# Row sum by an accumulating addition, squares on ScalarE, more transposes by DMA, the last tile in two halves, and a new order

## The chip, the cores and the metric

The kernel runs on one core of a Trainium2 chip. Its time is the device time in microseconds (us). The four compute engines are TensorE (PE in the profile, with its weight loads as PEld), VectorE (DVE), ScalarE (ACT) and GpSimd (POOL); SyncE (SP) issues most of the DMAs.

## What is computed

Inputs are r, k and v of shape (4 batches, 8 heads, 768 steps, 48), decays w and bonuses u per head and channel, and the weights of a two-layer network. The first part is a linear attention with a decaying state, the second a normalised network with a residual:

```python
for t in range(S):
    cur = np.einsum('bhd,bhe->bhde', u[None] * kt, vt)
    y[:, :, t] = np.einsum('bhd,bhde->bhe', rt, state + cur)
    state = w[None, :, :, None] * state + np.einsum('bhd,bhe->bhde', kt, vt)
# x: y as (B, S, H * D) = (4, 768, 384)
mu = np.mean(x, axis=-1, keepdims=True)
var = np.mean((x - mu) ** 2, axis=-1, keepdims=True)
xn = (x - mu) / np.sqrt(var + 1e-06) * g_ln
ch = np.maximum(xn @ w_ch1, 0.0) @ w_ch2        # 384 -> 1536 -> 384
return (x + ch).astype(np.float32)
```

## The kernel before

The 3072 rows (4 x 768) are cut into 24 tiles of 128 rows, six to a batch. A tile i passes through these steps, each a small function of the program whose name stands in the plan:

- `LK`, `LR`, `LV` (L315 to L322) load the tile's k, r and v, each 192 KB in runs of 192 bytes, through SP's queue into rings of ten buffers.
- `SK`, `SR` (through `times`, L203) scale k and r by powers of the decay into bf16 (`sck`, `scr`); `CV` casts v into `vv`.
- `TR` (L338) transposes `scr` and `sck` on TensorE, four 128x128 blocks each, into a PSUM tile `tr`; `TC`, or `TCr` and `TCk` apart, copies it to `trs` (r in half 0, k in half 1). For tiles in `K_BY_DMA` (18 to 23) only r is transposed so, and `TKD` (L477) brings k with a DMA transpose from `sck` to `trs`, issued on SP's queue.
- `Q` multiplies the two halves of `trs`; `AT` (L357) makes the 128x128 products of k and r per head; `AM` masks them into `A`; `S` (L388 to L401) makes the bonus terms and the state's increment; `CC`, `ZU`, `ZD` update the state `Z`; `VB` (L420) multiplies v by the bonus terms; `Y` (L430, L438) is the attention's output in PSUM. For tiles in `ZPE` (1 to 3) the old state is added in `S` by one matmul with the identity (L395), and then `ZU` alone makes the new state; otherwise `ZU` adds on VectorE and `ZD` multiplies on GpSimd.
- `X` (L445) adds `Y` and `Vb` to `x`. `ST` (L448) and `AG` (L452) take mean and variance of its rows; `XN` (L458, L460) writes mean minus x as bf16 into `xn`; `RS` (L466, L469) makes the inverse standard deviation on GpSimd.
- `LT` (L482) transposes `xn` on TensorE in three blocks and `XT` copies the result to `xT`.
- `UP` (L497) multiplies by the first weights, `RL` (L513, L515) applies the relu into `hT`, `DN` (L525) multiplies by the second weights, four matmuls of 384 columns to a step and three steps to a tile; `OT` (L535) scales and adds x, and `STO` (L542) stores 192 KB.

`GROUPS` says how many tiles share one pass of `UP`: one for tiles 0 to 7 and 20 to 23, two for 8 to 19. A step `UP,i` or `RL,i` belongs to group i // 16 and block i % 16; a step `DN,i` to tile i // 4.

At the start `LN`, `WBM`, `FK`, `FR` make the powers of the decay (`Fk`, `Fr`), `LG` loads the gain vector and `UGC` negates it, `LW1` and `IW2` load the two weight matrices in three parts each, and `SW` casts parts of the first to bf16 with the gain in them. `WU` and `DU` are matmuls of zeros that do no work of the reference.

The order of everything is one list, `PLAN`. It is walked from left to right; each entry is a step, its number and an engine letter (v VectorE, s ScalarE, g GpSimd, - where the step has only one). An engine runs its own instructions in this order, and waits on semaphores where a step needs another engine's result. SP's queue is one such order as well: loads, DMA transposes and stores stand in it one behind the other. In the listing of the program a DMA on it also waits for the landing of an earlier one, since eight semaphores are used in turn for DMAs issued by SP and ScalarE.

```python
for step in PLAN.split():
    name, i, e = step.split(",")
    steps[name](int(i), e)
```

Of the kernel before, what the change touches and what calls it, by code (L numbers as in the profile page):

```python
# [7 lines left out]
FP32 = mybir.dt.float32  # L8
# [87 lines left out]
def kernel(  # L96
# [347 lines left out]
    def X(i, e):  # L444
        nc.vector.tensor_tensor(out=xx(i)[:], in0=psum["y", i][:, :C], in1=Vb(i)[:], op=ALU.add)  # L445

    def ST(i, e):
        nc.vector.bn_stats(out=stats[i % 4][:], in_=xx(i)[:])  # L448

    def AG(i, e):  # L450
        g, j, _ = group_of[i]
        nc.vector.bn_aggr(out=mv[g][:, j, :], in_=stats[i % 4][:])  # L452
# [130 lines left out]
```

## Time and profile before

Three runs took 156.22, 157.09 and 157.25 us; the median is 157.09 us. The profile is of another execution of the same program:

| | |
|---|---|
| the profiled execution's own time | 156.55 us |
| its span, from the first instruction to the last | 154.4 us |
| outside the span | 2.15 us |
| PE, DVE, ACT, POOL busy | 146.4, 119.4, 76.2, 95.7 us |
| mean granted TensorE clock | 0.996 |
| matmuls | 1926, of them 105 of zeros |

"Busy" is the time in which at least one instruction of the engine was running. Matmuls overlap each other, so their own durations (219 ns for one of 128 columns) are longer than the distance at which they follow each other; that distance is read from the chain of waits or from the timeline, where eight transposes take 0.45 us. Lines of a helper (L198, L200, L203) stand for several steps, which the tile names tell apart.

### The profile page before, as it was taken

What the parts mean: (1) busy time and instruction counts of PE and PEld (TensorE: products, weight loads), DVE (VectorE), ACT (ScalarE), POOL (GpSimd) and SP (SyncE); (2) the same over time, 40 slices, a digit from 0 to 9 for tenths busy, and PEclk for the clock granted to TensorE, in tenths of its full rate; (3) what the DMA queues carried; (4) which work ended last, traced back from release to release, by engine and by line L of the source; (5) the groups of instructions that cost most, each with busy time, mean ns of one, the idle gap of its engine ahead of it and who ended that gap; (6) DMA issues with size and microseconds to landing.
All of it is one profiled execution on the core that took longest, in us unless ns stands there. A gap on an engine that the chain in (4) does not pass through costs nothing.

```text
span 154.4 us, 4697 instructions
## 1 busy us (share of the span) xinstructions
PE 146.4 (95%) x1926; PEld 118.6 (77%) x1926; DVE 119.4 (77%) x242; ACT 76.2 (49%) x149; POOL 95.7 (62%) x135
## 2 busy tenths in 40 slices
PE   7689999999899999999999999999999999999990
PEld 4488788868677887979688878877778778878770
DVE  2256989789998999999999999797797769734211
ACT  4526884434155747657535746356455244143330
POOL 3182665356749499995693698798766968333200
PEclk9999999999999999999999999999999999999998
DMA  4999999999999999989899897132153051102111
GB/s 82 192 182 354 349 200 206 210 177 212 226 200 188 199 255 179 257 170 232 170 243 208 176 261 107 51 89 34 51 87 87 0 89 51 51 20 82 56 56 51
DMA packets 84487, 23.51 MB, mean 152 GB/s; under 512 B 79857, under 2 KB 82930, under 8 KB 84466
## 3 DMA queue, kind: packets, MB, share of 16 engines
q1 hardware_dynamic: 83202, 22.03, 64.5%
q0 software_dynamic: 432, 1.18, 4.2%
q8 instruction: 15, 0.25, 0.7%
q10 hardware_dynamic: 832, 0.00, 0.3%
q14 instruction: 6, 0.05, 0.1%
HBM read 18.88 MB, written 4.72 MB: 153 GB/s over the span
## 4 chain that ended last, share of the span: by engine, by line
PE 73%; DVE 16%; DMA 3%; ACT 2%; issue 2%; SPq 1%; POOL 1%; POOLq 0%; DVEq 0%; ACTq 0%
PE o L525 27%; PE hp L497 26%; PE tr L338 5%; PE at L357 4%; DVE A L367 4%; DMA rf<-in_r_dram 3%; PE tr L482 3%; DVE scr L203 2%; PE y L438 2%; PE s L401 2%; PE y L430 2%; PE o L261 2%; DVE x L445 2%; PE s L388 1%; DVE stats L448 1%
## 5 line engine op out<-in xcount | busy, mean ns | idle before, releaser
L513 ACT ACTIVATE hT<-hp 128x512 bf16<-128x512 f32 x68 | 40.0, 597 | 49.5 <-PE hp L497 48.9
L497 PE MATMUL hp<-xT,w_sb 128*128 128x128 bf16 (+1 forms) x648 | 57.2, 237 | 0.3 <-ACT w_sb L306 0.2
L525 PE MATMUL o<-w_sb,hT 128*128 128x384 bf16 x288 | 57.1, 326 | 0.2 <-DVE hT L515 0.2
L497 PEld LDWEIGHTS <-w_sb 128*128 128x128 bf16 x648 | 49.4, 113 | 4.4 <-ACT w_sb L306 0.4
L525 PEld LDWEIGHTS <-hT 128*128 128x128 bf16 x288 | 25.3, 98 | 11.6 <-DVE hT L515 0.4
L367 DVE TENSOR_TENSOR A<-at,mask 128x1024 bf16<-128x1024 f32 (+1 forms) x26 | 29.1, 1127 | 3.3 <-PE at L357 3.3
L420 POOL TENSOR_TENSOR Vb<-vf,cc 128x384 f32<-128x384 f32 x24 | 21.6, 898 | 12.6 <-ACT cc L198 6.7
L203 POOL TENSOR_TENSOR scr<-rf,Fr 128x384 bf16<-128x384 f32 x16 | 16.2, 1019 | 11.7 <-DMA rf<-in_r_dram 8.2
L535 DVE SCALAR_TENSOR_TENSOR ot<-o,rs,x 128x384 f32<-128x384 f32 x24 | 14.7, 611 | 10.3 <-PE o L525 10.2
L445 DVE TENSOR_TENSOR x<-y,Vb 128x384 f32<-128x384 f32 x24 | 13.1, 547 | 4.2 <-POOL Vb L420 3.1
L203 POOL TENSOR_TENSOR Z<-ZS,WLZ 128x384 bf16<-128x384 f32 x13 | 13.6, 1048 | 2.5 <-DVE ZS L414 2.3
L198 ACT COPY trs<-tr 128x512 bf16<-128x512 bf16 (+1 forms) x13 | 10.0, 782 | 10.5 <-PE tr L338 10.5
L448 DVE BATCH_NORM_STATS2 stats<-x 128x6 f32<-128x384 f32 x24 | 13.3, 554 | 0.4
L203 POOL TENSOR_TENSOR sck<-kf,Fk 128x384 bf16<-128x384 f32 x12 | 12.6, 1046 | 0.3 <-PE s L401 0.3
L469 POOL TENSOR_TENSOR rs<-rs,expo 128x1 f32<-128x1 f32 (+1 forms) x18 | 10.9, 603 | 1.5
L338 PE MATMUL tr<-ident,scr 128*128 128x128 bf16 x96 | 9.7, 227 | 1.9 <-POOL scr L203 1.9
L261 PE MATMUL o<-warm 128*128 128x128 bf16 x105 | 10.3, 269 | 1.0 <-DVE warm L226 1.0
L203 DVE TENSOR_TENSOR sck<-kf,Fk 128x384 bf16<-128x384 f32 x12 | 9.6, 799 | 1.4 <-DMA kf<-in_k_dram 1.4
L203 DVE TENSOR_TENSOR q<-trs 128x512 bf16<-128x512 bf16 x18 | 8.8, 489 | 2.4 <-ACT trs L198 2.4
L261 PEld LDWEIGHTS <-warm 128*128 128x128 bf16 x105 | 8.7, 124 | 2.4 <-issue 1.3
L458 ACT ACTIVATE xn<-x,mv 128x384 bf16<-128x384 f32 x15 | 9.2, 613 | 2.5 <-DVE mv L452 2.5
L357 PE MATMUL at<-trs 48*128 48x128 bf16 x192 | 9.8, 222 | 0.4 <-DVE trs L200 0.3
(66 smaller groups left out, 180.2 us busy)
## 6 DMA issues: line engine op xcount, KB each, us to landing
kf<-in_k_dram SPq DMA_DIRECT2D x24, 192.0 KB, 3.9
vf<-in_v_dram SPq DMA_DIRECT2D x24, 192.0 KB, 4.1
rf<-in_r_dram SPq DMA_DIRECT2D x24, 192.0 KB, 3.9
out_dram<-ot SPq DMA_DIRECT2D x24, 192.0 KB, 2.5
w_f<-in_moe_w_ch_dram SPq DMA_DIRECT2D x3, 768.0 KB, 7.3
w_sb<-in_moe_w_ch_dram POOLq DMA_DIRECT2D x3, 384.0 KB, 6.5
trs<-sck SPq DMA_TRANSPOSE x6, 3.6
u_p<-in_u_dram ACTq DMA_DIRECT2D x2, 0.8 KB, 3.1
```

Of the source, the lines that this page charges most:

```text
L203: engines[e].tensor_tensor(out=out, in0=in0, in1=in1, op=ALU.mult)
L261: nc.tensor.matmul(out=warm_ps[0][:, :P], lhsT=warm[:], rhs=warm[:], start=True, stop=True)
L338: nc.tensor.transpose(out=t[:, a * HP + q, :], in_=flat[:, q, :], identity=ident[:])
L357: nc.tensor.matmul(out=t[:, par, q, :], lhsT=trs(i)[p0 : p0 + D, 1, q, :], rhs=trs(i)[p0 : p0 + D, 0, q, :], start=True, stop=True,)
L367: nc.vector.tensor_tensor(out=AA(i)[:, a:b].rearrange("p e q t -> p (e q) t"), in0=psum["at", i][:, a:b].rearrange("p e q t -> p (e q) t") ...
L420: nc.gpsimd.tensor_tensor(out=Vb(i)[:].rearrange("p (h d) -> p h d", h=H), in0=vf(i)[:], in1=cc(i)[:].unsqueeze(2).to_broadcast([P, H, D]) ...
L445: nc.vector.tensor_tensor(out=xx(i)[:], in0=psum["y", i][:, :C], in1=Vb(i)[:], op=ALU.add)
L448: nc.vector.bn_stats(out=stats[i % 4][:], in_=xx(i)[:])
L497: nc.tensor.matmul(out=t[:, a * gw : (a + 1) * gw], lhsT=w1_sb[n][kc][:, fb::FB], rhs=xT(g)[:, kc, :gw], start=(kc == 0), stop=(kc == CK - 1),
L513: nc.scalar.activation(out=o, in_=s, func=ACT.Relu)
L525: nc.tensor.matmul(out=psum["o", i][:, :C], lhsT=hT(g)[:, fk, j * P : (j + 1) * P], rhs=w2_sb[d][:, a, :], start=(fk == 0), stop=(fk == FK ...
L535: nc.vector.scalar_tensor_tensor(out=ot(i)[:], in0=psum["o", i][:, :C], scalar=rs[g][:, j : j + 1], in1=xx(i)[:], op0=ALU.mult, op1=ALU.add,)
```

## The change

Five things change, and with them the order of nearly every step.

1. `X` becomes one instruction that adds and also sums its rows into `sm`; `ST` and `AG` are gone. `XN` works with the row sum, so it writes C times what it wrote (C = 384), and the new step `SQ` on ScalarE squares that and sums it into `sq`; `RS` is made from `sq`, with the same factor C in it.
2. `K_BY_DMA` begins at 14 and not at 18; a new step `TRD` brings r by DMA for tiles 20 to 23 too, and their `TR` is gone from the plan; rows 14 to 23 of `xn` are brought to `xT` by DMA (`LTD`), and their `LT` and `XT` are gone.
3. `ZPE` takes in tile 4.
4. The last tile's `DN`, `OT` and `STO` are each cut into two halves of 192 columns: `DA`, `DB`, `OA`, `OB`, `SA`, `SB`. `DB` writes a PSUM tile of the ring of `UP`.
5. The plan is another list: steps stand elsewhere, and many have another engine. By count: `SR` has 9 on GpSimd and 15 on VectorE (16 and 8 before), `SK` 10 and 14 (12 and 12), `TC` 8 on ScalarE and 4 on VectorE (6 and 10, of 16), `Q` 9 on GpSimd (6), `XN` 8 on VectorE, 12 on ScalarE, 4 on GpSimd (3, 15, 6), `CV` 16 on ScalarE (13). The zero matmuls are 94 (105). `LG` and `UGC` stand near the front.

```diff
-ZPE = [1, 2, 3]
-K_BY_DMA = [18, 19, 20, 21, 22, 23]
+ZPE = [1, 2, 3, 4]
+K_BY_DMA = [14, 15, 16, 17, 18, 19, 20, 21, 22, 23]
...
     def X(i, e):
-        nc.vector.tensor_tensor(out=xx(i)[:], in0=psum["y", i][:, :C], in1=Vb(i)[:], op=ALU.add)
-
-    def ST(i, e):
-        nc.vector.bn_stats(out=stats[i % 4][:], in_=xx(i)[:])
-
-    def AG(i, e):
+        nc.vector.scalar_tensor_tensor(
+            out=xx(i)[:], in0=psum["y", i][:, :C], scalar=1.0, in1=Vb(i)[:], op0=ALU.mult, op1=ALU.add,
+            accum_out=sm[i][:],
+        )
+
+    def SQ(i, e):
         g, j, _ = group_of[i]
-        nc.vector.bn_aggr(out=mv[g][:, j, :], in_=stats[i % 4][:])
+        nc.scalar.activation(
+            out=sqj[:], in_=xx(i)[:], func=ACT.Square, bias=sm[i][:], scale=-float(C), accum_out=sq[g][:, j : j + 1]
+        )
...
         if e == "s":
-            nc.scalar.activation(out=xn(i)[:], in_=xx(i)[:], func=ACT.Identity, bias=mean, scale=-1.0)
+            nc.scalar.activation(out=xn(i)[:], in_=xx(i)[:], func=ACT.Identity, bias=sm[i][:], scale=-float(C))
...
         nc.gpsimd.tensor_scalar(
-            out=rs[g][:], in0=mv[g][:, :, 1], scalar1=1e-6, scalar2=1.0, op0=ALU.add, op1=ALU.mult
+            out=rs[g][:], in0=sq[g][:], scalar1=1.0 / C, scalar2=1e-6 * C * C, op0=ALU.mult, op1=ALU.add
         )
...
+    def TRD(i, e):
+        flat = scr(i)[:].rearrange("p h d -> p (h d)")
+        nc.sync.dma_start_transpose(out=trs(i)[:, 0], in_=flat)
...
+    def half(i, name, pool, c0):
+        g, j, _ = group_of[NT - 1]
+        n = FK // NW
+        if i == 0:
+            psum[name] = pool.tile([P, 512], FP32, name="o" if name == "oA" else "hp")
+        for a in range(n):
+            fk = i * n + a
+            nc.tensor.matmul(
+                out=psum[name][:, : C // 2],
+                lhsT=hT(g)[:, fk, j * P : (j + 1) * P],
+                rhs=w2_sb[i][:, a, c0 : c0 + C // 2],
+                start=(fk == 0),
+                stop=(fk == FK - 1),
+            )
...
+    def half_out(i, name, c0):
+        g, j, _ = group_of[i]
+        nc.vector.scalar_tensor_tensor(
+            out=ot(i)[:, c0 : c0 + C // 2], in0=psum[name][:, : C // 2], scalar=rs[g][:, j : j + 1],
+            in1=xx(i)[:, c0 : c0 + C // 2], op0=ALU.mult, op1=ALU.add,
+        )
...
+    def half_store(i, c0):
+        b, c = divmod(i, NCH)
+        nc.sync.dma_start(
+            out=out[b, c * L : (c + 1) * L, c0 : c0 + C // 2], in_=ot(i)[:, c0 : c0 + C // 2]
+        )
```

`LTD` was in the program before, but no plan entry used it:

```python
def LTD(i, e):
    g, j, _ = group_of[i]
    nc.sync.dma_start_transpose(out=xT(g)[:, :, j * P : (j + 1) * P], in_=xn(i)[:])
```

The beginning of the new plan, up to the first `UP`, and its end:

```
MW,0,v WF,0,- TL,0,s MI,0,g WU,13,- MM,0,g MP,0,v LN,0,s LG,0,- ROWSI,0,s WBM,0,- LR,0,-
UGC,0,s FK,0,s LK,0,- FR,0,s LR,1,- SR,0,g WL,0,s SK,0,v LK,1,- UW,0,g DU,24,- TR,0,-
SR,1,v LK,2,- TCk,0,v SK,1,v LV,0,- TCr,0,v SK,2,v DU,12,- AT,0,- LR,2,- TR,1,- CV,0,s
AMa,0,v LV,1,- Q,0,g AMb,0,v SR,2,v LW1,0,- DU,7,- Y,0,- S,0,- TCk,1,v CC,0,s TCr,1,v
CV,1,s ZU,0,v Q,1,g DU,10,- TR,2,- LV,2,- TC,2,v DU,4,- AT,1,- VB,0,g S,1,- SW,2,s
AMa,1,v LW1,1,- SW,1,g SW,0,s X,0,v Q,2,v CV,2,g XN,0,s AMb,1,v DU,20,- LT,0,- CC,1,v
SQ,0,s Y,1,- ZU,1,v LK,3,- VB,1,g AT,2,- XT,0,v SW,5,s SW,4,v RS,0,g UP,0,- LR,3,-
...
STO,17,- DN,74,- SQ,21,s Q,23,g AT,22,- LTD,21,- OT,18,v RL,226,s UP,224,- RS,15,g AM,22,v DN,76,-
RL,224,s UP,240,- ZU,22,v STO,18,- DN,77,- ZD,22,g DN,78,- S,23,- UP,225,- OT,19,v Y,22,- CC,23,v
RL,225,s VB,23,g DN,80,- X,22,v RL,240,s DN,81,- STO,19,- AT,23,- DN,82,- XN,22,v SQ,22,s AM,23,v
UP,241,- RS,16,g UP,242,- OT,20,v LTD,22,- RL,241,s Y,23,- DN,84,- X,23,v RL,242,s DN,85,- XN,23,v
STO,20,- UP,256,- DN,86,- SQ,23,s LTD,23,- UP,257,- RL,256,s RS,17,g OT,21,v UP,258,- RL,257,s DN,88,-
RL,258,s DN,89,- STO,21,- UP,272,- DN,90,- RL,272,s UP,273,- UP,274,- OT,22,v RL,273,s DA,0,- RL,274,s
DA,1,- DA,2,- DB,0,- STO,22,- DB,1,- OA,23,v DB,2,- OB,23,v SA,23,- SB,23,-
```

## The prediction

> **What bounds the kernel now.** I read the page's busy times first, then the engines by stage, then what TensorE waits for, and last the two ends of the timeline.
>
> ```profile
> PE 146.4 (95%) x1926; PEld 118.6 (77%) x1926; DVE 119.4 (77%) x242; ACT 76.2 (49%) x149; POOL 95.7 (62%) x135
> ```
>
> The table by stage (stretch, then busy us and instructions of PE, PEld, DVE, ACT, POOL, clock, DMA share, GB/s):
>
> ```profile
> 31.00:60.00 29.00, 28.44 (x434) 22.64 (x433) 27.14 (x51) 14.63 (x31) 20.52 (x26) 1.00 0.98 206
> 60.00:78.00 18.00, 17.78 (x251) 14.40 (x250) 17.62 (x35) 10.73 (x22) 14.72 (x19) 1.00 0.97 205
> 78.00:96.00 18.00, 18.00 (x229) 15.15 (x226) 17.81 (x35) 10.53 (x18) 13.24 (x17) 1.00 1.00 204
> 96.00:120.00 24.00, 24.00 (x289) 19.42 (x287) 19.07 (x39) 12.90 (x27) 18.21 (x25) 1.00 0.27 64
> 120.00:151.00 31.00, 30.88 (x368) 24.08 (x365) 16.68 (x33) 10.41 (x21) 13.87 (x20) 1.00 0.18 50
> ```
>
> From 31 us on PE is full. DVE is nearly as full until 96 us, ScalarE is half idle, and the DMA engines fall from full to a quarter once the loads are done. Who released PE after 31 us (total, times, longest):
>
> ```profile
> PE at L357 <- DVE trs L200: 0.3, 1, 0.3
> PE y L438 <- DVE A L367: 0.2, 1, 0.2
> PE o L525 <- DVE hT L515: 0.2, 1, 0.2
> ```
>
> So 0.7 us of named waits in 120: there a TensorE instruction taken away is time gained, and one that has to wait is time lost. A busy PE can hide small gaps, since matmuls overlap: by starts in the timeline I find about 1.1 us more between 39.7 and 42.8, where the chain of waits runs through DVE. Before 31 us it is different (start, duration, engine, instruction, count, idle before it):
>
> ```profile
> 4.35 0.58 ACT L275 ACTIVATE Fk<-y,pow_i 128x384 f32<-128x384 f32 x1 [1.80 <-PE y L271]
> ...
> 7.09 0.99 POOL L203 TENSOR_TENSOR scr<-rf,Fr 128x384 bf16<-128x384 f32 x1 [5.01 <-DMA rf<-in_r_dram]
> ...
> 8.13 0.61 PE L338 MATMUL tr<-ident,scr 128*128 128x128 bf16 x4 [1.85 <-POOL scr L203]
> ...
> 17.97 0.62 ACT L458 ACTIVATE xn<-x,mv 128x384 bf16<-128x384 f32 x1 [0.71 <-DVE mv L452]
> ...
> 19.43 0.83 PE L497 MATMUL hp<-xT,w_sb 128*128 128x128 bf16 x12
> ```
>
> The first transpose waits for r of tile 0, the first `UP` for tile 0's whole attention. At the other end the last `DN` ends at 150.9, and `OT` (0.62) and a store follow. DMA transposes, from the view of `trs` on SP:
>
> ```profile
> L477 SPq DMA_TRANSPOSE trs<-sck x6: 1190/1212/1947, 92.3 to 123.8; - x6
> ...
> DMA to landing us min/median/max: 2.4/3.6/4.3
> ```
>
> SP is held for 1.2 us by each; it lands 2.4 us after its issue starts if the queue is quiet, 3.6 beside a store, 4.3 beside the loads (the first, at 92.3).
>
> **The change part by part, against the profiled execution (156.55 us).**
>
> TensorE work. Gone are k's transposes of tiles 14 to 17 (16), r's of 20 to 23 (16) and ten tiles of three in `LT` (30): 62. Eight take 0.45 us in the chain, so 56 ns each: 62 x 0.056 = -3.5. Tile 4 in `ZPE` adds one matmul of 384 columns, 0.16 (four of them take 0.65): net **-3.3**. 24 half matmuls of `DA`, `DB` replace 12 whole ones at the same number of columns: 0. The zero matmuls all stand before the PE-bound stage; their removal is in the start's sum.
>
> DVE. Gone: 24 `ST` at 554 ns and 24 `AG` at 173, 17.4 us. `X` turns from 547 ns to the form of `OT`, 611: +1.5. Seven more `SR` at 766: +5.4, two `SK` at 799: +1.6, five `XN` at 597: +3.0; six fewer `TC` at 678 and six fewer `XT` at 356: -6.2; three fewer `Q` at 489: -1.5. The row sum's read-out is not in the trace. The Trainium skill ("VectorE: DVE Perf Modes", section "Two Vector instructions with no wait between them") says that an operation which also writes out its accumulator is two instructions. Nearest rows of one column: 60 ns (a memset) and 173 (`AG`); I take 100, so +2.4; without the rule it would be 0, both hidden. Sum about -11 of 119: DVE no longer runs level with PE. Cover: PE is the later of the two from 31 us, so this is worth only the gaps around 40 us. I take **-0.5** (0 to -1.1).
>
> ScalarE. 24 `SQ` at the price of `XN` (613 ns), plus a read-out between 0 and 204 ns (the small `g_neg` row of that engine): 15 to 20 us. The moves of other steps about cancel, so 76 becomes 91 to 96 of 150: its cover is the half that is idle, 48.9 us of it spent by `RL` waiting for `UP`. An `SQ` in front of an `RL` can hold it for 0.7 us, and `UP` two blocks later needs that buffer; there is mostly a `DN` (0.65) between. Taken as 0 (-0 to +1.5). GpSimd loses some 8 us net; it had 38% idle: 0.
>
> The start. `LG` is now second on SP's queue and `UGC` stands before `FK` on ScalarE. The gain vector's DMA lands after 3.2 us by its row: issued near 1.1, landed 4.3, so `FK` starts at 4.5 instead of 4.35, a loss of 0.15; `FR` and `SR` of tile 0 are behind it. r of tile 0 is now the first big load, not the third: issued near 1.6, with the median of 3.9 landed at 5.5. `SR,0` then starts at 5.6 instead of 7.09. 24 zero matmuls from 4.2 at 0.11 each end at 6.8, so the first `TR` is at 6.8 instead of 8.13. `X` to `XN` loses `ST` and `AG`, 0.7 us on the path. But ahead of `XN,0` ScalarE now does two casts of weights that arrive behind eight loads, as before: not before about 14.7, plus 1.3. So `XN,0` is near 16.3 and the first `UP` near 17.8 instead of 19.43. Then something else is late: `IW2,0` stands on POOL's queue behind `SK,3`, which waits for k of tile 3. It is issued near 20 instead of 15.65; at 5.1 to 6.5 us to landing that is 25 to 26.5, while the first `DN`, with 2.3 us more PE work in front of it, would be ready at 24.2. That gives back some of it: **-1.3** (+0.5 to -2.5).
>
> The rows by DMA. `LT` and `XT` became `LTD`: 1.2 us of SP and 2.4 to 4.3 to landing. The first `UP` of the group waits for it, in order, with all of PE behind it. The PE work in the plan between `XN` and that `UP`: tile 15 three `DN`, `TR` of r, `AT`, `Y`, `S` = 1.95 + 0.22 + 0.33 + 0.37 + 0.27 = 3.1; likewise 17: 3.4, 19: 3.2, 20: 4.2, 21: 3.0, 22: 3.0, 23: 4.0. In the trace of before the real distance is 0.3 to 0.8 longer than counted so (tile 23: 1.47 counted, 142.36 to 144.13 in the timeline); with 0.5 the margins are 3.6, 3.9, 3.7, 4.7, 3.5, 3.5, 4.5. Needed: `XN` 0.6, a semaphore, and the landing: 3.05 quiet, 4.25 beside a store, 4.95 beside loads. Quiet nothing is lost; beside stores 0.6 + 0.3 + 0.6 + 0.8 + 0.7 = 3.0; tiles 14 to 17 fall where loads still come. I take **+2.0** (0 to +4).
> Here a rule speaks against the change. The skill's section "The three transpose paths" of the same page gives 1309 ns for a 128x128 block by DMA and 390 by TensorE. Block by block three would be 3.9 us, an estimate, and seven groups would lose 0.65 + 3.9 against their margins, 4.6 us in all; then nothing of the PE gain stays. The six rows here are of four blocks and land in 2.4 when quiet, so blocks overlap; I take the trace.
> K and r by DMA (`TKD`, `TRD`) have 4.6 to 21 us of PE work between `SK` or `SR` and `AT`: 0. SP carries 24 transposes now, 29 us against 7. Late on it are the stores behind a waiting `LTD`; none but the last matters, and three `ot` buffers give two tiles of room.
>
> The end. `DA,2` needs `RL,274`, which ends about 0.85 after the last `UP`; `DA,0` and `DA,1` cover 0.65 where two full `DN` covered 1.3: **+0.2**. `OA` and its store lie under `DB`. The last addition has 192 columns: from the `A` rows (1208 for 1024 columns, 682 for 512) a column costs 1.03 ns, so 611 becomes 0.41, and the smaller store saves perhaps 0.2: **-0.4**.
>
> Sum: -3.3 - 0.5 - 1.3 + 2.0 + 0.2 - 0.4 = **-3.3**, so 153.25 for an execution like the profiled one. That lies 0.54 under the median of the three runs; counted from the median it would be 153.8. I forecast **153.3**.
>
> **The rivals.**
> *Everything lands in time* (0.18). Transposes land in 2.4, the start gives 2.5, the gaps at 40 us close: -3.3 - 2.5 - 1.1 - 0.2 = -7, about 149.8. For it: after 96 us the DMA share is 0.27. Against: `STO` and `LTD` alternate on SP.
> *Rows by DMA come late* (0.09), the other side. If `LTD` lands after 4.3 us throughout, the seven groups lose 1.3 + 1.0 + 1.2 + 0.3 + 1.5 + 1.4 + 0.5 = 7.2 against a gain of 5.3 from the rest: +1.9, about 158.7. It decides from a mean landing of about 4.0 us. For it: the first of the six took 4.3, and three times as many now share SP. Against: two took 2.4.
> *The start gives nothing and the rows cost 3 to 4* (0.11): -3.3 - 0.7 + 3.5 = about -0.5, or 156.5. For it: the second weights' part is issued 4 us later.
> *The forecast* (0.62): 151 to 155.5.
>
> **The numbers.** A measurement of this kernel tells 1%, 1.6 us, from no change. Faster by over 1% (under 155.5): forecast and first rival, 0.80. Within 1%: 0.11. Slower: 0.09. The range, 149.8 to 156.6, cuts off about a tenth on each side.
>
> **What would show it.** Right: transposes on PE fall from 240 to 178; first `UP` near 17.8; `ST` and `AG` gone and DVE's busy time near 108; ScalarE's above 90; waits of PE for `LTD` before the first `UP` of a group, 0.3 to 1 us each, summing to 2. Wrong: landings of transposes near 4.3 after 105 us; a first `UP` later than 19; `RL` behind `SQ` named as what released `UP`; gaps before the first `DN` over 2 us.

## The result, and the profile after

Four runs of the changed kernel took 154.45 to 155.46 us, median 154.95; the kernel before, beside them, 157.17. The ratio is 0.9869, with a 95% interval from 0.9824 to 0.9914: 2.2 us faster. In the experiments below the same program gave 0.9886 [0.9858, 0.9915] over 22 runs. The forecast was 153.3; the measured time is 1.65 us above it, inside its case (151 to 155.5) and its range. By the wider set the gain is 1.8 us (1.14% of 157.8).

Not all of this lies in the program's own instructions. The time outside the span is 2.08 to 2.23 us in every execution of the kernel before, and 1.73 to 1.94 in every one of the changed kernel and of all its variants, old statistics or old order included. So about 0.36 us of the gain (2.14 less 1.78, the means) belongs to no term of the forecast, and its cause stays open; inside the span the gain is about 1.4 to 1.9 us.

The profiled execution after took 155.46 us, its span 153.7. It is the slowest of the four, and the profiled one before was faster than its median, so this pair of profiles shows only 1.1 us of the 2.2. Executions of one program differ by 3% and more here: the ratios compare only the fast ones, while the profiles of c_before, iw2_early and mid_mend are of slower executions and serve for single intervals, not for their length.

Busy times of the page, changed kernel:

```profile
PE 143.1 (93%) x1866; PEld 115.1 (75%) x1866; DVE 106.4 (69%) x220; ACT 88.7 (58%) x190; POOL 87.5 (57%) x126
```

VectorE fell from 119.4 to 106.4 us, ScalarE rose from 76.2 to 88.7, and PE fell by 3.3. The groups of instructions (count, busy us and mean ns, idle time ahead) give the new operations' prices:

```profile
L450 ACT ACTIVATE sqj<-x,sm 128x384 bf16<-128x384 f32 x24 | 14.7, 613 | 4.2 <-DVE x L443 3.9
...
L443 DVE SCALAR_TENSOR_TENSOR x<-y,Vb 128x384 f32<-128x384 f32 x24 | 13.2, 552 | 4.6 <-POOL Vb L418 2.7 <-PE y L436 1.6
...
L450 ACT ACTIVATION_READ_ACCUMULATOR sqj<-x,sm 128x1 f32 x24 | 4.6, 190 | 0.0
...
L443 DVE DVE_READ_ACCUMULATOR x<-y,Vb 128x1 f32 x24 | 2.0, 82 | 0.0
...
L558 DVE SCALAR_TENSOR_TENSOR ot<-hp,rs,x 128x192 f32<-128x192 f32 x1 | 0.4, 419 | 0.5 <-PE hp L542 0.5
```

The addition with a row sum takes 552 ns, no more than the plain addition (547), plus 82 for reading out the accumulator. The squares take 613 plus 190 on ScalarE. The last addition of 192 columns takes 419.

By stage (us, then busy and instructions of PE, PEld, DVE, ACT, POOL, clock, DMA share, GB/s):

```profile
31.00:60.00 29.00, 28.88 (x419) 22.98 (x418) 22.91 (x42) 18.36 (x39) 17.46 (x23) 1.00 0.93 199
60.00:78.00 18.00, 16.62 (x227) 13.17 (x225) 14.82 (x28) 12.92 (x29) 13.18 (x19) 1.00 0.99 203
78.00:96.00 18.00, 17.92 (x218) 14.78 (x217) 13.78 (x28) 12.70 (x28) 12.05 (x14) 1.00 0.95 202
96.00:120.00 24.00, 24.00 (x277) 19.04 (x276) 20.17 (x41) 15.08 (x36) 13.23 (x18) 1.00 0.56 122
120.00:151.00 31.00, 29.55 (x367) 23.26 (x365) 13.75 (x28) 13.05 (x26) 13.21 (x20) 1.00 0.33 87
```

PE is full again from 31 to 60 and from 78 to 120 us, but no longer from 60 to 78: 16.62 of 18, where it had 17.78. The DMA engines are as full as before until 96 us. After it they now carry the rows as well (0.56 and 0.33 against 0.27 and 0.18). What PE waited for (total, times, longest):

```profile
PE o L527 <- DMA w_sb<-in_moe_w_ch_dram: 1.1, 1, 1.1
...
PE tr L484 <- ACT xn L456: 1.0, 1, 1.0
...
PE hp L499 <- DMA xT<-xn: 0.8, 1, 0.8
...
PE o L527 <- DVE ot L583: 0.7, 1, 0.7
```

The first line is the first `DN` at 26 us, the second the `LT` of tile 0 at 16, the third the rows of tile 21 at 132, the last a `DN` at 64. From the timeline of the start (start, duration):

```profile
4.41 0.58 ACT L273 ACTIVATE Fk<-y,pow_i 128x384 f32<-128x384 f32 x1
...
5.54 1.00 POOL L201 TENSOR_TENSOR scr<-rf,Fr 128x384 bf16<-128x384 f32 x1 [3.46 <-ACT Fr L276]
...
6.77 0.63 PE L336 MATMUL tr<-ident,scr 128*128 128x128 bf16 x4
...
15.44 0.60 ACT L456 ACTIVATE xn<-x,sm 128x384 bf16<-128x384 f32 x1
...
17.06 0.86 PE L499 MATMUL hp<-xT,w_sb 128*128 128x128 bf16 x12
...
26.04 0.82 PE L527 MATMUL o<-w_sb,hT 128*128 128x384 bf16 x4 [1.12 <-DMA w_sb<-in_moe_w_ch_dram]
```

The first transpose (6.77) and `XN` of tile 0 (15.44) come as forecast or earlier, and the first `UP` starts at 17.06 instead of 19.43. The first `DN` starts at 26.04; before it was 23.74.

A span hides small gaps, so I measured PE by starts: for each instruction the distance to the next one's start, less the distance usual for its kind (the 20th percentile in the same profile). What is left over is called a stall; the rest is work, the zero matmuls included. It is my arithmetic on the traces, for both profiles of each program, and a kind drawn a little differently (by line and shape) moves single figures by up to 0.8 us. About 7 us of every column are no stall at all: the eight `AT` products of a tile, 0.33 us in the chain, follow in pairs 3 ns apart, so that percentile counts next to nothing for them. Only differences between columns are read:

| us | before | c_before | changed | c_after |
|---|---|---|---|---|
| work of PE | 129.80 | 129.85 | 126.63 | 126.37 |
| stalls, 0 to 30 | 9.58 | 11.86 | 9.12 | 9.13 |
| stalls, 30 to 60 | 3.54 | 6.62 | 3.38 | 4.29 |
| stalls, 60 to 100 | 3.91 | 4.35 | 6.03 | 5.40 |
| stalls, 100 to the end | 2.66 | 3.10 | 3.89 | 3.80 |

The work fell by about what was forecast; 11 fewer zero matmuls at 56 ns, 0.6 us, are in that fall. Stalls rose where PE had been full: by 1.0 to 2.1 between 60 and 100 us and by 0.7 to 1.2 after that. The chain of waits, taken from 60 to 80 us, shows of what kind they are (its summary by line, which the view cuts off at the end). Before:

```profile
by line: DVE scr L203 14.2%; PE o L525 13.5%; PE hp L497 13.5%; DVE A L367 9.6%; issue 6.2%; DVE x L445 4.6%; DVE vv L200 3.9%; ACT hT L513 3.7%; PE at L357 3.3%; DVE trs L200 3.0%; PE y L438 2.8%; DVE q L203 2.8%; DVE ZS L414 2.7%; DVE ot 
```

And after:

```profile
by line: DMA kf<-in_k_dram 24.8%; POOL Vb L418 13.2%; DVE A L365 11.4%; SPq L314 7.0%; PE hp L499 6.6%; issue 6.2%; SPq L317 6.0%; DVE xn L458 5.4%; SPq L320 3.8%; POOL vv L198 3.5%; DVE sck L201 2.9%; DVE vv L198 2.9%; DVE x L443 2.8%; POO
```

Before, no DMA stands in this stretch, neither in this profile nor in the second one: the chain goes through VectorE and PE. After, 4.95 of 20 us are the landing of one k tile (4.24 in c_after), and another 3.35 (the SPq entries) are SP issuing loads one behind the other.

### The profile page after: what moved, and what is told of

Same layout as the page of the kernel before. It is cut to its first block, busy times and chain, and to the rows that moved or that the text cites. A ratio compares the mean times of both kernels' runs of the same rounds, so it can differ in the third digit from the quotient of the medians.

```text
span 153.7 us, 4643 instructions
## 1 busy us (share of the span) xinstructions
PE 143.1 (93%) x1866; PEld 115.1 (75%) x1866; DVE 106.4 (69%) x220; ACT 88.7 (58%) x190; POOL 87.5 (57%) x126
## 4 chain that ended last, share of the span: by engine, by line
PE 54%; DMA 21%; DVE 9%; SPq 6%; issue 3%; POOL 3%; ACT 1%; DVEq 0%; ACTq 0%; POOLq 0%
PE o L527 22%; PE hp L499 21%; DMA kf<-in_k_dram 11%; DMA w_sb<-in_moe_w_ch_dram 4%; DVE A L365 3%; DMA vf<-in_v_dram 3%; DMA xT<-xn 3%; PE at L355 2%; PE tr L336 2%; SPq L320 2%; POOL Vb L418 2%; PE y L436 2%; SPq L317 2%; PE s L399 1%; PE y L428 1%
## 5 line engine op out<-in xcount | busy, mean ns | idle before, releaser
L527 PE MATMUL o<-w_sb,hT 128*128 128x384 bf16 x276 | 53.9, 326 | 2.0 <-DMA w_sb<-in_moe_w_ch_dram 1.1
L450 ACT ACTIVATE sqj<-x,sm 128x384 bf16<-128x384 f32 x24 | 14.7, 613 | 4.2 <-DVE x L443 3.9
L443 DVE SCALAR_TENSOR_TENSOR x<-y,Vb 128x384 f32<-128x384 f32 x24 | 13.2, 552 | 4.6 <-POOL Vb L418 2.7
L201 POOL TENSOR_TENSOR sck<-kf,Fk 128x384 bf16<-128x384 f32 x10 | 10.0, 1008 | 9.3 <-DMA kf<-in_k_dram 6.3
L201 POOL TENSOR_TENSOR scr<-rf,Fr 128x384 bf16<-128x384 f32 x9 | 9.8, 1091 | 8.8 <-DVE q L201 5.1
L201 POOL TENSOR_TENSOR q<-trs 128x512 bf16<-128x512 bf16 x9 | 10.9, 1215 | 6.7 <-DVE trs L198 4.0
L201 POOL TENSOR_TENSOR Z<-ZS,WLZ 128x384 bf16<-128x384 f32 x12 | 12.0, 1004 | 2.3 <-DVE ZS L412 2.3
L196 ACT COPY trs<-tr 128x1024 bf16<-128x1024 bf16 (+1 forms) x12 | 10.4, 866 | 3.2 <-PE tr L336 3.2
L201 DVE TENSOR_TENSOR scr<-rf,Fr 128x384 bf16<-128x384 f32 x15 | 8.8, 599 | 1.8 <-DMA rf<-in_r_dram 1.6
L196 ACT CAST vv<-vf 128x384 bf16<-128x384 f32 x16 | 8.2, 510 | 3.1 <-DMA vf<-in_v_dram 2.3
```

Of the source, the lines that this page charges most:

```text
L196: nc.scalar.copy(out=out, in_=in_)
L201: engines[e].tensor_tensor(out=out, in0=in0, in1=in1, op=ALU.mult)
L443: nc.vector.scalar_tensor_tensor(out=xx(i)[:], in0=psum["y", i][:, :C], scalar=1.0, in1=Vb(i)[:], op0=ALU.mult, op1=ALU.add, accum_out=sm[ ...
L450: nc.scalar.activation(out=sqj[:], in_=xx(i)[:], func=ACT.Square, bias=sm[i][:], scale=-float(C), accum_out=sq[g][:, j : j + 1])
L527: nc.tensor.matmul(out=psum["o", i][:, :C], lhsT=hT(g)[:, fk, j * P : (j + 1) * P], rhs=w2_sb[d][:, a, :], start=(fk == 0), stop=(fk == FK ...
```

## The experiments

Line numbers of kernels with an edited plan differ by a few from those of the changed kernel.

### Both kernels once more

**c_after**, unchanged:

> The changed kernel once more, for the comparison of what runs beside it, and for a second profile, since the first one is of the slowest of its four executions (155.46 us against a median of 154.95). Ratio to before near 0.987. If the stalls of PE between 60 and 80 us (3.5 us in the first profile) belong to the order, they come again within 0.3 us; if they belonged to that one execution, they are nearer to the 2.2 us of before, and the span is near 152.9.

Ratio 0.9886, and the profile's span 153.6. The stalls of 60 to 80 us were 2.9, where I had expected 3.5 again or the 2.2 of before: half of the surplus came again, at the same places. PE waits for the `DN` of tile 7 (0.7 in both), an `AT` (0.3) and a `Y` (0.3). These belong to the order; from 60 to 100 us the two profiles have 6.0 and 5.4.

**c_before**, unchanged:

> The kernel before once more, unchanged, for a second profile of it: all comparisons of stalls so far rest on one. If that profile is typical, PE's stalls are again near 9.6 us up to 30 us, 3.5 from 30 to 60, 3.9 from 60 to 100 and 2.7 from 100 to 150, each within 0.6, and the last matmul starts within 1 us of 150.6. If not, the difference is what a stage of a single profile can be trusted to.

A single execution of 162.78 us, not typical: its first `DN` waited 2.1 us for the second weights, and 5.4 of its 6.2 us of extra stalls lie ahead of 60 us. From there on its stalls agree with the first profile within 0.45 us. A stage after 60 us can be read from one profile to about half a microsecond; the start can't.

### Rows by DMA or by TensorE

**rows_pe**: all ten `LTD` become `LT` and `XT` on VectorE; two copies of r move up.

```diff
-LTD,18,- RL,197,s
+LT,18,- XT,18,v RL,197,s
...
-DN,86,- SQ,23,s LTD,23,- UP,257,- RL,256,s
+DN,86,- SQ,23,s LT,23,- UP,257,- XT,23,v RL,256,s
```

> Rows 14 to 23 go back to TensorE (30 transposes in LT, 10 copies in XT, all on VectorE), in the order of the changed kernel; two copies of r stand a few steps earlier so that the one PSUM tile of the transposes is free. PE's work grows by 30 x 56 ns = 1.7 us. Theory 3 (the transposes by DMA cost only the waits seen in the profile, 0.9 to 1.2 us): this kernel is 0.5 to 0.8 us slower than the changed one. The prediction's sum (they cost 2.0 us): 0.3 us faster. If ten fewer transposes on SP also bring loads and stores earlier, it is faster by more than that, and the landings of the loads after 90 us show it.

Ratio 0.9998 [0.9971, 1.0025]: the whole gain is gone, 1.8 us (1.1% of 157.8) against the changed kernel beside it. PE's work rose by 1.6, and this order, written for DMAs, gained a few stalls with the copies (98 to 102 us). So ten rows by DMA are worth about the PE time they save, in an order written for them; that is more than the 0.5 to 0.8 that I expected of this run. The prediction charged them 2.0 us against 1.7 saved, which is too much by 1 to 2 us. The other 32 transposes (k and r), tile 4 in `ZPE` and the halves of the last tile were not taken back one by one.

**sto18_late**: the one wait for rows that is left, tile 21, was put down to a store beside it.

```diff
-UP,240,- ZU,22,v STO,18,- DN,77,- ZD,22,g DN,78,- S,23,- UP,225,- OT,19,v
+UP,240,- ZU,22,v DN,77,- ZD,22,g DN,78,- S,23,- UP,225,- OT,19,v
...
-STO,19,-
+STO,19,- STO,18,-
```

> The changed kernel with the store of tile 18 behind that of tile 19 on SP's queue, so that no store is issued while the rows of tile 21 are being transposed. Theory (a DMA transpose beside a store lands in 3.6 to 3.9 us instead of 2.3, as the prediction had it from one row of before): the rows of tile 21 land 2.3 to 2.6 us after their issue, and PE's wait of 0.7 to 0.9 us in front of the first UP of that tile is gone. Rival (that transpose is late for another reason): it takes 3.6 to 3.9 again and PE waits again. The rows of tile 22 may meet two stores now: if they do, they take over 3 us.

A single execution, 155.15 us. No store was issued in that flight, and the wait stayed:

```profile
128.70 2.58 SPq L466 DMA_TRANSPOSE xT<-xn  x1
...
132.47 0.86 PE L494 MATMUL hp<-xT,w_sb 128*128 128x128 bf16 x12 [0.58 <-DMA xT<-xn]
```

These are the issue of the transpose and the `UP` that waited for it. The view of the DMA engines over the same 4.4 us, in 40 slices (the second line: queue, packets, MB, share of the time), shows that the rows were not alone:

```profile
DMA  9100000800007994000000100000000000000000
...
q8 instruction: 1, 0.02, 2.0%
```

The transpose's burst is over by 130.4 us (the digits 7994), but a trickle of its packets ends only near 131.5, and a 16 KB packet of another queue, "instruction", lies between. For comparison the rows of tile 22 in the changed kernel, without such a packet:

```profile
DMA  0000000000000000003999982000000000000000
...
xT<-xn SPq DMA_TRANSPOSE x1, 2.3
```

One compact burst, landed after 2.3 us (the last figure). In every profile of the changed order with these rows, a code packet of 16 KB falls into the flight of the rows of tile 21 (in five of them at 130.5, 129.9, 129.5, 130.7, 131.2 us), so this tile alone can't separate the two. The other transposes can. Over all 14 kept profiles, take those with no load issued in the 4 us ahead of them or in their flight:

| no load near | transposes | issue to landing, us |
|---|---|---|
| a code packet starts within 2.2 us of the issue | 5 | 3.38 to 4.48 |
| no such packet | 134 | 2.29 to 3.18, median 2.42 |
| of these, a store issued in the 1 us ahead or in the flight | 99 | median 2.41 |

The trace of before, from which the prediction read "3.6 beside a store", shows the same. Its transpose at 113.4 us, which has a store just ahead of it, over the 2.8 us from its issue:

```profile
q8 instruction: 1, 0.02, 2.1%
...
trs<-sck SPq DMA_TRANSPOSE x1, 3.9
```

The packet starts 1.48 us after the issue; 1.26 us after it at 123.8 (landing 3.6), and 1.3 at 92.3 (4.3). The two that landed in 2.4 have none. So the store is refuted as the cause, here and in the prediction. That a code packet makes a landing late rests on these coincidences: no run took a packet away.

### The start

**iw2_early**:

```diff
-SK,3,g XN,1,s LW1,2,- UP,1,- RL,0,s SR,3,v LT,1,- IW2,0,g
+IW2,0,g SK,3,g XN,1,s LW1,2,- UP,1,- RL,0,s SR,3,v LT,1,-
```

> The first part of the second weights is issued ahead of the scaling of k of tile 3 on GpSimd, so some 2 us earlier. Theory 1 (the start's lead of 2.4 us at the first UP is lost because that part is issued late): it lands at 24 to 24.5 instead of 26.0, the first DN starts 1.0 to 1.5 us earlier and the kernel is about 1 us faster than the changed one (ratio to before about 0.981). Rival (the DMA engines are full, and what one transfer gains the next ones lose): the first weights' last part, 21.3 in the first profile, lands about 1 us later, the UP steps that need it wait as much longer, and the time is that of the changed kernel within 0.3 us.

The first part was issued 1.3 us earlier (17.86) and landed at 25.76 instead of 26.0; the first weights' last part landed at 22.2 instead of 21.5. These landings are what the rival said. The time, 0.9851 [0.9787, 0.9915], settles nothing: the interval holds theory 1's 0.981 as well as the changed kernel's 0.9886.

**start_mend**:

```diff
-SK,3,g XN,1,s
+IW2,0,g IW2,1,g SK,3,g XN,1,s
...
-LR,6,- UP,48,- SK,4,g OT,0,v UP,50,- LR,4,- DN,4,- SR,6,v
+UP,48,- SK,4,g OT,0,v UP,50,- LR,4,- DN,4,-
...
-LK,6,- SK,5,v
+LK,6,- LR,6,- SK,5,v
...
-SR,5,v DN,10,-
+SR,5,v SR,6,v DN,10,-
```

> The changed kernel with the first two parts of the second weights issued ahead of the scaling of k of tile 3, and with r of tile 6 loaded (and scaled) later, so that one load less shares the DMA engines with the weights. If the start is held by the bytes that the DMA engines bring before the first DN (theory 5), the last part of the second weights lands 0.5 to 1 us earlier than 30.1, the first DN starts 0.5 to 1 us earlier than 26.05 and the kernel is 0.4 to 0.8 us faster than the changed one. If it is held by the place of the issue on GpSimd (theory 1), the first part lands at 24.5 or earlier and the gain is over 1 us. If neither, the time is the same within 0.3 us.

```profile
17.95 1.33 POOL L306 DMA_DIRECT2D w_sb<-in_moe_w_ch_dram  x2
...
25.41 0.82 PE L522 MATMUL o<-w_sb,hT 128*128 128x384 bf16 x4
```

The second weights are issued earlier, and the first `DN` starts at 25.41 without a wait; the last part landed at 29.45 instead of 30.1. Theory 5 has the landings right: the earlier issue and one load less ahead of the weights, both in this run, bring them 0.65 us forward. But the time did not follow: 0.9921 [0.9888, 0.9955], if anything slower than the changed kernel. New stalls came up in front of `TR` of tile 4 (37 us, 0.5) and of an `UP` that waits for rows (102, 1.1). From 4 to 30 us the DMA engines are busy throughout in both kernels (a share of 1.08 before, 1.12 after), so what is served first makes another late; that this is the limit of the start is argued from the shares and from these two runs, not shown by one that carries fewer bytes.

### The loads and VectorE from 30 to 100 us

**sto_late**:

```diff
-SR,4,v STO,0,- DN,6,-
+SR,4,v DN,6,-
...
-LV,7,- CC,4,s
+LV,7,- STO,0,- CC,4,s
```

> The store of tile 0 stands behind six more loads on SP's queue, so that the queue no longer stops from 27.6 to 31.8 us until the addition of tile 0 is done. Theory 2 (the hole in the loads behind this store is what PE pays for at 60 to 80 us): the loads of k of tiles 12 to 14 land 2 to 4 us earlier, DVE's and GpSimd's waits for k of 4.0 and 3.7 us fall under 1.5, PE's stalls from 60 to 80 us fall from 3.5 to about 2.2, and the kernel is about 1 us faster than the changed one (ratio about 0.981). Rival A (those stalls come from DVE's own order and lengths): the loads come earlier and the stalls stay, time the same within 0.3 us. Rival B (the loads that start earlier share the engines with the second weights): the first DN starts 0.5 to 1 us later and the time is the same or worse.

Ratio 0.985 [0.9809, 0.9891]: not to be told from the changed kernel (0.9886), and the 0.981 of theory 2 lies at its very edge. The hole closed, k of tile 6 landed 2.3 us earlier (32.9 against 35.2) and GpSimd's longest wait for k fell from 3.7 to 1.3. But from 60 us on the loads landed where they had (k of tile 12 at 69.2, in the changed kernel at 68.9), and the stalls there stayed (6.6 us). So the store's place isn't the cause; whether earlier loads would help, which theory 2 and rival A differ on, this run doesn't test. One expectation rested on a misreading: VectorE's wait for k of 4.0 us, which I took from the list of waits, is its first scaling at 6 us. A list of waits has no places; the timeline has.

**mid_mend**:

```diff
-DN,26,- SQ,8,s LV,14,- TR,11,- XN,8,v CC,9,s OT,6,v VB,9,g
+DN,26,- SQ,8,s LV,14,- TR,11,- OT,6,v XN,8,v CC,9,s VB,9,g
...
-AM,7,v LK,17,- CV,7,s
+AM,7,v LK,12,- CV,7,s
...
-RL,98,s LR,17,- DN,24,-
+RL,98,s LR,12,- DN,24,-
...
-X,8,v LK,19,- AM,9,v
+X,8,v LK,13,- AM,9,v
...
-TC,11,s LR,12,- AT,10,-
+TC,11,s LR,17,- AT,10,-
...
-RL,114,s LK,13,- AM,10,v
+RL,114,s LK,19,- AM,10,v
...
-XN,9,s LK,12,- XT,8,v
+XN,9,s LK,17,- XT,8,v
```

> The changed kernel with two swaps in its order: on VectorE the step OT of tile 6 stands ahead of XN of tile 8, and on SP's queue k of tiles 12 and 13 and r of tile 12 change places with k of 17 and 19 and r of 17, which stood ahead of them. Theory 4 (the stalls between 60 and 80 us come from the new order: DN of tile 7 waits 0.9 us for OT behind XN, and S of tile 11 0.4 us for a VectorE that stands waiting for k): these two stalls fall under 0.2 us, VectorE's and GpSimd's waits for k under 1 us each, and the kernel is 0.8 to 1.2 us faster than the changed one (ratio near 0.982). Rival (the slack is taken up at the next wait, since VectorE is late there anyway): stalls move on, 0.3 us or less is gained.

The stall at 64 us, in c_after:

```profile
63.76 0.83 POOL L418 TENSOR_TENSOR Vb<-vf,cc 128x384 f32<-128x384 f32 x1 [0.35 <-ACT cc L196]
...
63.89 0.92 DVE L458 TENSOR_SCALAR xn<-x,sm 128x384 bf16<-128x384 f32 x1
...
64.73 0.60 DVE L583 SCALAR_TENSOR_TENSOR ot<-o,rs,x 128x384 f32<-128x384 f32 x1
...
65.38 0.81 PE L527 MATMUL o<-w_sb,hT 128*128 128x384 bf16 x4 [0.66 <-DVE ot L583]
```

`XN` of tile 8 runs on VectorE while GpSimd makes `Vb`, and takes 0.92 us; `OT` stands behind it, and `DN` of tile 7 needs the one PSUM buffer that `OT` frees. With the two exchanged:

```profile
63.62 0.83 POOL L413 TENSOR_TENSOR Vb<-vf,cc 128x384 f32<-128x384 f32 x1
...
63.75 0.60 DVE L578 SCALAR_TENSOR_TENSOR ot<-o,rs,x 128x384 f32<-128x384 f32 x1
...
64.27 0.41 DVE L453 TENSOR_SCALAR xn<-x,sm 128x384 bf16<-128x384 f32 x1
...
64.52 0.82 PE L522 MATMUL o<-w_sb,hT 128*128 128x384 bf16 x4
```

`DN` starts 0.33 us after `AT`, with no wait, and `XN`, with GpSimd nearly done, takes 0.41. The stall of 0.4 in front of `S` of tile 11 is gone too. But new ones came: 0.5 us at 67, 1.0 at 77, 0.6 at 101. The ratio is 0.9848 [0.9778, 0.9917], which holds the expected 0.982 too; the stalls from 60 to 100 us are 5.3, against 5.4 and 6.0, and that speaks for the rival. Note that k of tile 12 landed at 49.8 instead of 68.9: the one load that fills the chain above was 19 us early, and the stalls hardly fell.

**combo1** adds to it another engine for `XN` of tile 11, and moves one `UP`:

```diff
-DN,32,- XN,11,v STO,5,- SQ,11,s
+DN,32,- XN,11,s STO,5,- SQ,11,s
...
-UP,240,- ZU,22,v STO,18,- DN,77,- ZD,22,g DN,78,- S,23,-
+ZU,22,v STO,18,- DN,77,- ZD,22,g DN,78,- UP,240,- S,23,-
```

> The changed kernel with the two swaps of mid_mend, XN of tile 11 on ScalarE instead of VectorE, and the first UP of tile 21 behind two more DN steps of tile 19. Each takes one stall that the profile shows: 0.9 us before DN of tile 7, 0.4 before S of tile 11, 0.3 to 1.0 before the transposes of tile 11 and 0.3 behind them, 0.7 to 0.9 before UP of tile 21. Theory 4 (single waits of a misplaced step): PE's stalls from 60 to 100 us fall from 5.6 to about 4, and the kernel is 1.5 to 2 us faster than the changed one, ratio near 0.977. Rival (the stalls move to the next step): 0.5 us or less, ratio 0.985 or more.

**combo2** is combo1 with the plan edit of sto_late:

> As combo1, with the store of tile 0 behind six loads as in sto_late. If the hole in the loads at 28 to 32 us costs anything once the waits on VectorE are mended: 0.3 to 0.8 us faster than combo1. If the loads are ahead of their use from there on: the same within 0.3 us.

0.9868 [0.9817, 0.9919] and 0.9856 [0.9819, 0.9893]: no gain that can be told, and combo1's 0.977 is excluded. Each named stall vanished, and another stood in its place. The timeline of combo1 shows where the new one at 77 us begins:

```profile
73.79 0.50 POOL L193 CAST vv<-vf 128x384 bf16<-128x384 f32 x1 [0.95 <-DMA vf<-in_v_dram]
...
74.25 0.83 POOL L413 TENSOR_TENSOR Vb<-vf,cc 128x384 f32<-128x384 f32 x1
...
75.12 0.56 DVE L438 SCALAR_TENSOR_TENSOR x<-y,Vb 128x384 f32<-128x384 f32 x1 [1.47 <-POOL Vb L413]
...
75.72 0.62 ACT L451 ACTIVATE xn<-x,sm 128x384 bf16<-128x384 f32 x1 [0.53 <-DVE x L438]
76.24 0.60 ACT L445 ACTIVATE sqj<-x,sm 128x384 bf16<-128x384 f32 x1
...
76.88 0.48 ACT L191 COPY xT<-tr 128x384 bf16<-128x384 bf16 x1
...
77.41 0.33 PE L479 MATMUL tr<-ident,xn 128*128 128x128 bf16 x3 [0.84 <-ACT xT L191]
...
79.41 0.62 DVE L578 SCALAR_TENSOR_TENSOR ot<-o,rs,x 128x384 f32<-128x384 f32 x1 [1.55 <-DMA out_dram<-ot]
```

GpSimd stands waiting for v of tile 12, and `Vb` of tile 11 is queued behind that cast; VectorE's addition waits 1.47 us for `Vb`; `XN` and `SQ` of tile 11 follow late on ScalarE, the copy `XT` of tile 10 stands behind them there, and PE waits 0.84 for the PSUM tile that the copy frees. In mid_mend, with that `XN` still on VectorE, the transposes waited 0.83 for `XN` itself: the late addition costs PE the same on either engine. Two us later `OT` waits 1.55 for a store. At the head of each of these two strings stands a DMA. The v that GpSimd waits for is loaded behind v of tiles 16 and 17; it landed at 60.2 in the kernel before, and no run moved it. In combo2 the stalls from 60 to 100 us did fall to 4.4, the level of before (3.9 and 4.35), but 5.1 came after 100.

### The statistics alone, and the order without them

**before_stats** puts the first part of the change into the kernel before:

```diff
-X,0,v SW,6,s DU,13,- AT,2,- Q,2,v Y,1,- CV,2,g ST,0,v AG,0,v LW1,0,- CC,1,s XN,0,s RS,0,g
+X,0,v SW,6,s DU,13,- AT,2,- Q,2,v Y,1,- CV,2,g LW1,0,- CC,1,s XN,0,s SQ,0,s RS,0,g
```

> The kernel before with only the first part of the change: the row sum from the addition's accumulator, the squares on ScalarE directly behind the step XN, no ST and AG; order, transposes and last tile as before (RS of three groups stands later, behind the squares it now needs). PE's work is unchanged, DVE's falls by some 14 us. If relief of DVE is worth the 0.5 us that the prediction gave it: ratio 0.997, and the stalls of PE near 40 us shrink. If squares in front of the relu on ScalarE cost something: ratio 1.003 or more. The bonus at the start (X to XN shorter by 0.7 us) would add at most 0.4.

Ratio 1.0143 [1.0087, 1.02]: 2.2 us slower, although VectorE lost 9.6 us of busy time (119.4 to 109.8; I had expected 14). VectorE's relief, bought with squares on ScalarE, is worth less than nothing there. In GpSimd's waits stands one thing that replaced it:

```profile
POOL rs L459 <- ACT sqj L445: 18.0, 9, 3.2
```

`RS` on GpSimd now waits for squares that ScalarE reaches in its turn behind relus and copies: 18.0 us in nine waits, where it waited 5.3 for `AG` in the kernel before. Casts, `Vb` and the issue of weights are queued behind `RS`. The last two parts of the second weights are issued from 21.89 instead of 20.44, behind a cast that waits for the first weights, and a `DN` at 29.5 us has a stall of 1.0. How much of the 2.2 us is due to `RS` was not separated.

**after_oldstats** keeps the new order and takes the statistics back:

```diff
-X,4,v DN,13,- LR,7,- AM,5,v SQ,4,s XN,4,g
+X,4,v ST,4,v AG,4,v DN,13,- LR,7,- AM,5,v XN,4,g
```

> The changed kernel with the old statistics (ST and AG on VectorE directly behind each X, no squares on ScalarE): DVE's work grows by some 15 us in the new order, ScalarE's falls by some 19. If DVE is off the path in the new order as the prediction has it, about 0.5 to 1 us slower than the changed kernel (ratio to before near 0.993). If the new order lives on DVE's relief (its stalls of PE between 60 and 80 us all come from a late DVE): 2 us slower or more, ratio 1.002 or higher, with PE's stalls from 60 to 100 us rising from 5.6 us to over 7.5.

Ratio 1.0207 [1.0161, 1.0252]: 3.2% of 157.8, 5.1 us slower than the changed kernel. PE's waits, in part:

```profile
PE tr L480 <- ACT xn L452: 2.0, 3, 1.1
...
PE y L432 <- DVE A L361: 1.4, 3, 0.6
...
PE o L523 <- DVE ot L579: 1.2, 2, 0.8
```

The stalls went up in every stage (9.9, 4.8, 6.6, 5.9), most after 100 us, not between 60 and 100 as I had expected. They are waits for `A`, `OT` and `XN`, so for VectorE or what follows it: the new order has VectorE do more scalings and `XN`, and with the statistics back on it (120.6 busy) it is late in every stage. `ST` and `AG` stand directly behind `X` here; an order written for them would lose less.

So the two parts don't add: statistics alone +1.4%, order and DMAs without them +2.1%, both together -1.1%.

## Why the prediction held, and where it was off

The range held, but in part by luck: the errors below have both signs. Rows by DMA cost 1.1 to 1.4 us less than charged, and 0.36 us came from outside the span; against that stand 0.8 us at the start, about 1 us of waits for ScalarE and 1.45 to 1.95 us of new waits for VectorE between 60 and 100 us. A further 0.5 of the 1.65 us is the base: 153.3 was counted from an execution 0.54 us under its median. The terms overlap, so they do not add up exactly.

Each term of its sum against what was measured:

| term | forecast | measured |
|---|---|---|
| PE's work | -3.3 | -3.2, -3.4 (two profiles, zero matmuls in it) |
| VectorE's relief | -0.5 | waits of PE for it, 30 to 60 us: -0.95, -0.45; 60 to 100 us: +1.95, +1.45 |
| ScalarE | 0 | waits of PE for it, 46 to 74 us: +0.95, +1.04 |
| the start | -1.3 | stalls to 30 us: -0.5, -0.5 |
| rows by DMA | +2.0 | one wait, 0.8 and 0.6 |
| k and r by DMA | 0 | one wait of VectorE, 0.9; none of PE |
| the end | +0.2 - 0.4 | 0 to +0.1 |

**PE's work** is right: transposes fell from 240 to 178, at 55 to 56 ns from start to start, and a half matmul follows the next at 82 ns where a whole one takes 162. That is -3.5 + 0.16; the table's figure agrees within what its arithmetic can tell.

**VectorE** is the step that failed. Its durations were right in sum (-13 against -11), and the cover as well ("PE is the later of the two from 31 us"). The gaps near 40 us that it priced at 0.5 did close: the waits of PE that end on VectorE from 30 to 60 us (those over 0.1 us, by starts) come to 0.95 before and to 0 and 0.50 in the two profiles after. But the step then took PE to stay full with VectorE relieved, and asked only what a relief is worth, not what the new order would hang on next. It hung on VectorE again, 20 us later: from 60 to 100 us such waits come to 0.39 before and to 2.34 and 1.84 after, which is nearly the whole rise of the stalls there. They end on `A`, `OT`, `ZS` and `XN`, the longest, 0.73, on an `OT` behind an `XN`. What makes VectorE late there is only argued. In the order after, k of tile 12 is loaded behind k of 17 and 19, and lands in the moment VectorE needs it (68.9 us; 59.5 before); the DMA engines are as full as before until 96 us (0.99 and 0.95). The chain from 60 to 80 us holds no DMA before and 4.95 us of landing after. Yet with k of tile 12 early (mid_mend, combo1) the stalls moved on and hardly fell, so this load alone is not the cause; other loads (v of tile 12), the place of single steps and GpSimd's `Vb` stay as candidates, and no run frees the DMA engines.

**ScalarE** was taken as 0, and its cover (the idle half) did not hold everywhere: PE waits for `XN` (0.15), a cast (0.16), a copy (0.16) and two relus (0.26 and 0.22), all between 46 and 74 us, where no wait of PE over 0.1 us ended on ScalarE before. The feared order, a relu behind a square, is not among them: one relu stood behind a cast that waited for v, the other behind an `XN`, and only the copy behind a square. That is within the term's range (up to +1.5), and it takes back what the gaps at 40 us gave: the stalls from 30 to 60 us are 3.4 and 4.3, 3.5 before.

**The start**: the mechanism was right, the size not. The first `UP` came even earlier than forecast (17.06 against 17.8), the second weights' first part was issued at 19.26 and landed at 26.0 as worked out (near 20, and 25 to 26.5). But the part given back was taken too small: in the first profile of each kernel PE had lost 16.4 us by its first `DN` (its start less the work on tiles done by then): the changed one had 2.3 us more work behind it and started 2.3 us later. iw2_early and start_mend suggest why: with the DMA engines busy throughout, a part that is issued earlier makes another land later.

**Rows by DMA**: the sign of the argument against the rule was right: blocks overlap, and the median landing is 2.3 us, not 3.9. The size was off because a late landing was put down to a store beside it (3.0 of the sum's losses): with a store beside them and no code packet, transposes land in 2.41 us (median of 99). The margins were met nearly everywhere; of the five groups that were to meet a store only one waited, and not for a store.

**The end**: from the start of the last two `UP` to the end of the last addition it is 4.17 us before and 4.15 after; to the end of the span 6.98 and 7.06. The short addition was priced right (0.41 against 0.42), and `DA,2` waited 0.19 for its relu, as forecast (0.2). The smaller store's gain did not appear.

**Signs to look for**: VectorE near 108 (106.4) came about, ScalarE above 90 just not (88.7); waits for `LTD` of 0.3 to 1 us in sum 2 did not. Of the rivals, "everything in time" was wrong in that new gaps opened where others closed, and "rows late" in the landings, which after 105 us stayed at 2.3 to 2.9 but for tile 21.

The rivals' figures are not all counted from one base either: 156.55 - 0.5 is 156.05, not 156.5, and 156.55 - 7 is 149.55.

Between the spans of the profiles the change is -0.7 to -0.8, and between the medians -1.8 to -2.2. The difference is the profile of before, which stands 0.5 to 1.2 us under the medians of its own program, and the 0.36 us outside the span.

## What to carry to other kernels

When work is taken from the busiest engine, look at what stands behind it in the new order before pricing the relief: here a scaling, an addition or a copy that still comes late, some of them behind loads of far tiles, with the DMA engines full. An order and the durations it was written for belong together: each half of this change alone made the kernel slower. A stall removed was worth nothing here as long as the chain over that stretch was not followed to its end. And before a late transfer is put down to what stands beside it in the queue, the other queues are worth reading: here the late ones met a code packet, and those that met only a store were not late.

## What the runs showed of the hardware

- A DMA transpose of three or four blocks mostly lands 2.3 to 2.5 us after its issue once the loads are done, with or without a store beside it, and in the changed kernel mostly 2.8 to 3.9 beside loads. With a 16 KB code packet in its flight and no load near it took 3.4 to 4.5 (five of them). The rows of tile 16, with a load ahead of them, took 3.8 to 4.3 in the five profiles where a packet starts 1.7 to 2.1 us after their issue, 2.5 and 2.8 in two where it starts later, and 2.3 to 2.4 in the three where none falls into the flight. The `UP` behind the rows of tile 21 started 3.7 to 3.9 us after their issue. The Trainium skill ("Runtime: NRT & Kernel Launch", section "Instruction fetch mechanics") has instructions refilled in 16 KiB blocks by a DMA queue of their own; the trace agrees on the queue and the size (14 such packets of 0.9 to 1.5 us each).
- `XN` on VectorE takes 0.41 us with GpSimd idle. Where a GpSimd instruction on a whole tile was already running, it ends 0.21 to 0.22 us after that one's end: 0.92 us (tile 8), 1.15 (tile 11), 0.76 (tile 15) in the changed kernel, 0.41 in mid_mend, where `Vb` had 0.18 left. Where `Vb` started 0.16 us after it (tile 21), it took 0.41. `OT`, with one operand in PSUM, takes 0.60 to 0.62 throughout.
- The accumulator's read-out is an instruction of its own: 82 ns on VectorE, 190 on ScalarE.
